# Windowed attention with sinks, then a gated MLP block: half of the spatial weights turned by DMA, and another PSUM bank for one unit

## The chip, the cores and the metric

The kernel runs on one core of one Trainium2 chip. The time is the device time of one launch in microseconds (us), and lower is better. Several executions are timed; one more is recorded by the hardware profiler, and every view of the profile below is of that one execution.

The engines have short names: PE is TensorE (matmuls and transposes), PEld its weight loads, DVE is VectorE, ACT is ScalarE, POOL is GpSimd, and SP is SyncE, which in this kernel only issues DMAs. SPq is SP's queue.

## The reference

```python
# attention: B=4, H=8, S=768, D=64, 4 sink columns, window 128
scores = q @ k.T / sqrt(D)
keep   = (pos[None, :] < 4) | ((rel >= 0) & (rel < 128))     # rel = row - column
a      = softmax(where(keep, scores, -1e9))
x      = (a @ v).transpose(0, 2, 1, 3).reshape(B, S, 512)
# gated MLP
h      = gelu_tanh(x @ w_in)                  # 512 -> 1024
u, v   = h[..., :512], h[..., 512:]
v_n    = (v - mean(v)) / sqrt(var(v) + 1e-6) * g_ln
v_s    = einsum('ts,bsd->btd', w_sg, v_n) + b_sg[None, :, None]   # w_sg is 768 x 768
out    = x + (u * v_s) @ w_out
```

The spatial product sums over positions s. TensorE needs the summed index on the partitions, so w_sg, which is read with t on the partitions, has to be turned once: wsgT holds it with s on the partitions, as six blocks of 128 rows by 768 columns.

## The kernel before

All tiles have 128 partitions. S is six tiles (NT = 6, HT = 3). Attention is done for pairs of heads: 4 batches of 4 pairs are 16 pairs, n = 0 to 15 (HP = 4). The MLP is done for a batch ("block" b) when its four pairs are through.

The order of the work is written out by hand in the loop over n (line 571); each engine executes its own instructions in that order. In an iteration the scores of pair n are made in three groups g (`score`, line 249), exponentiated by ACT and masked by DVE (`keep_band`, line 266); meanwhile the value products of pair n - 1 are done (`values`), and the keys and queries of pair n + 1 are turned by PE (`keys`, `queries`). At the end of an iteration SP gets the loads of pair n + 3 (`load_qk`, line 75).

When n is a multiple of 4, `hidden` (line 424) runs the first half of the MLP of the batch just finished, n // 4 - 1: six units `hidden_v` (line 327), each four matmuls and a GELU on ACT, and statistics on DVE; then eight units `hidden_u` (line 339). What follows, the spatial products (`spatial`, eight units of six matmuls, line 376) and the projections (`project`, six units, line 391), is put into a list, `fillers`, and `spread` takes them out one or two at a time between the attention work of the next iterations. For block 0 the list begins with the six units `spatial_weights` (line 177) that turn w_sg. So this happens once, at n = 5. Of the eight spatial units the first four (n = 0 in the code of `spatial`) read the first 384 columns of wsgT and the last four the second 384.

w_sg is loaded at n = 4 by two DMAs of POOL's queue (line 168), the first for t tiles 0 to 2, the second for 3 to 5. For pairs 4 to 14 that are not the last of their batch, x is turned by a DMA transpose from SP's queue (line 321); otherwise by PE (`columns`, line 283).

PSUM has eight banks: `ps_s` for scores (two buffers of two banks), `ps_a` for values (one), `ps_t`, tag "tp", for the transposes of keys and queries (one), and `ps_m`, tag "mm", two buffers shared by everything else: `hidden_v`, `hidden_u`, `spatial`, `project`, `columns` and `spatial_weights`. A unit that takes a buffer waits until the unit before last in the same pool has been read out.

Of the kernel before, what the change touches and what calls it, by code (L numbers as in the profile page):

```python
# [8 lines left out]
F32 = mybir.dt.float32  # L9
# [8 lines left out]
def kernel(  # L18
# [14 lines left out]
    nc = tc.nc  # L33

    B, H, S, Dh = q.shape
# [5 lines left out]
    NT = S // 128  # L41
    HP = H // 2
# [13 lines left out]
    ps_t = ctx.enter_context(tc.tile_pool(name="ps_t", bufs=1, space=PSUM))  # L56
    ps_m = ctx.enter_context(tc.tile_pool(name="ps_m", bufs=2, space=PSUM))
# [3 lines left out]
    HT = NT // 2  # L61
# [13 lines left out]
    def load_qk(n):  # L75
        b, hp = divmod(n, HP)
        pair = []
        for src, name in ((k, "k_sb"), (q, "q_sb")):
            dst = loads.tile([128, 2, NT, 64], F32, name=name)
            nc.sync.dma_start(out=dst, in_=src[b, 2 * hp:2 * hp + 2].rearrange(  # L80
                "h (p t) d -> p h t d", t=NT))
            pair.append(dst)
        qk[n] = pair
# [71 lines left out]
    wsg_sb = consts.tile([128, NT, S], BF16, name="wsg_sb")  # L155
    w_out_sb = consts.tile([128, KU, DM], BF16, name="w_out_sb")
    wsgT = consts.tile([128, NT, S], BF16, name="wsgT")
# [16 lines left out]
            nc.gpsimd.dma_start(out=w_out_sb,  # L174
                                in_=moe_w_out.rearrange("(c p) f -> p c f", p=128))

    def spatial_weights(si):
        wps = ps_m.tile([128, NT, 128], BF16, name="wps", tag="mm")
        for ti in range(NT):
            nc.tensor.transpose(wps[:, ti, :],  # L180
                                wsg_sb[:, ti, 128 * si:128 * (si + 1)], iden)
        nc.vector.tensor_copy(wsgT[:, si, :], wps.rearrange("p t q -> p (t q)"))  # L182

    packed, qTs, exps, avs = {}, {}, {}, {}
    x_sb, xT = {}, {}
# [1 line left out]
    def repack(n, eng):  # L187
        packed[n] = []
        for src, name in zip(qk.pop(n), ("k_bf", "q_bf")):
            flat = work.tile([128, NT, 128], BF16, name=name)  # L190
            eng.tensor_copy(flat.rearrange("p t (h d) -> p h t d", h=2), src)  # L191
            packed[n].append(flat)
# [134 lines left out]
    def hidden_v(b, j):  # L327
        if j == 0:
            v_alls[b] = work.tile([128, NT, DF], F32, name="v_all", tag="v_all", bufs=1)
            mvs[b] = small.tile([128, NT, 2], F32, name="mv", bufs=2)  # L330
        h_ps = ps_m.tile([128, 512], F32, name="hv", tag="mm")
        for c in range(KD):
            nc.tensor.matmul(h_ps, xT[b][:, c, 128 * j:128 * (j + 1)],  # L333
                             w_in_sb[:, c, DF:], start=(c == 0), stop=(c == KD - 1))
        nc.scalar.activation(out=v_alls[b][:, j, :], in_=h_ps, func=AF.Gelu_apprx_tanh)  # L335
        st = small.tile([128, 6], F32, name="st")
        nc.vector.bn_stats(out=st, in_=v_alls[b][:, j, :])  # L337
        nc.vector.bn_aggr(out=mvs[b][:, j, :], in_=st)

    def hidden_u(b, f, n):  # L340
        if f == 0 and n == 0:
            uTs[b] = work.tile([128, KU, S], BF16, name="uT")
        h_ps = ps_m.tile([128, 512], F32, name="hu", tag="mm")
        for c in range(KD):
            nc.tensor.matmul(h_ps[:, 0:NH], w_in_sb[:, c, 128 * f:128 * (f + 1)],  # L345
                             xT[b][:, c, NH * n:NH * (n + 1)],
                             start=(c == 0), stop=(c == KD - 1))
        nc.scalar.activation(out=uTs[b][:, f, NH * n:NH * (n + 1)],  # L348
                             in_=h_ps[:, 0:NH], func=AF.Gelu_apprx_tanh)
# [3 lines left out]
    def inverse_root(b):  # L353
        rstd = rstds[b] = small.tile([128, NT], F32, name="rstd", bufs=2)
        var = small.tile([128, NT], F32, name="var", bufs=2)
        tmp = small.tile([128, NT], F32, name="tmp", bufs=2)
        nc.vector.tensor_scalar_add(var, mvs[b][:, :, 1], 1e-6)
        nc.vector.tensor_single_scalar(tmp.bitcast(I32), var.bitcast(I32), 1,
                                       op=ALU.logical_shift_right)
        nc.vector.tensor_scalar(out=rstd.bitcast(I32), in0=tmp.bitcast(I32),  # L360
                                scalar1=-1.0, scalar2=float(0x5F3759DF),
                                op0=ALU.mult, op1=ALU.add)
        for _ in range(3):
            nc.vector.scalar_tensor_tensor(out=tmp, in0=rstd, scalar=-0.5, in1=rstd,
                                           op0=ALU.mult, op1=ALU.mult)
            nc.vector.tensor_mul(tmp, tmp, var)
            nc.vector.scalar_tensor_tensor(out=rstd, in0=tmp, scalar=1.5, in1=rstd,
                                           op0=ALU.add, op1=ALU.mult)

    def normalise(b, j):  # L370
        if j == 0:
            vns[b] = work.tile([128, NT, DF], BF16, name="vn")
        nc.vector.tensor_scalar(out=vns[b][:, j, :], in0=v_alls[b][:, j, :],
                                scalar1=mvs[b][:, j, 0:1], scalar2=rstds[b][:, j:j + 1],
                                op0=ALU.subtract, op1=ALU.mult)
# [35 lines left out]
    def project_halves(b, t, queue):  # L411
        project(b, t, queue, nc.scalar, slice(DM // 2, DM))
        project(b, t, queue, nc.vector, slice(0, DM // 2))

    fillers = []
# [6 lines left out]
    def hidden(b, between, queue=nc.sync):  # L422
        def step():
            if between:
                between.pop(0)()

        for j in range(NT):
            hidden_v(b, j)
            for _ in range(min(j + 1, 2)):
                step()  # L430
        for i in range(2 * KU):
            hidden_u(b, i % KU, i // KU)
            if i == 0:
                inverse_root(b)
            elif i <= NT:
                normalise(b, i - 1)
        if b == 0 and queue is nc.sync:
            fillers.extend(lambda si=si: spatial_weights(si) for si in range(NT))
        for n in range(2):
            for f in range(KU):  # L440
                fillers.append(lambda f=f, n=n: spatial(b, f, n))
        for t in range(NT):
            if b == B - 1 and t == NT - 1:
                fillers.append(lambda t=t: project_halves(b, t, queue))
            else:
                by = nc.scalar if b == B - 2 else nc.vector
                fillers.append(lambda t=t, by=by: project(b, t, queue, by))
# [123 lines left out]
    for n in range(NP):  # L571
        if n + 2 < NP:
            repack(n + 2, G)
            load_v(n + 2)
        load_weights(n)
        late = half_valued == n - 1

        def value(i):
            if n > 0 and (i >= HT or not late):
                values(n - 1, i)  # L580

        points = (HT + 1) * ((HP - n) % HP)

        def spread(left):
            if n > HP * (B - 1):
                fill(1 if left > 2 or (left == 1 and n < NP - 1) else 0)
            else:
                fill(-(-len(fillers) // (points + left)))

        for g in range(HT):  # L590
            if g == HT - 1 and n % HP == 0 and n > 0:
                sinks(n)
            if n + g > 0:
                score(n, g)
            if g < 2 and not late:
                for i in range(HT * g, HT * (g + 1)):
                    value(i)
            if g == 0 and n > 0 and n + 1 < NP:
                keys(n + 1)
                if n < HP:  # L600
                    queries(n + 1, A, ps_m, "mm")
            if g == 0 and late:
                for i in range(HT, NT):
                    value(i)
                spread(HT + 1)
            if g == HT - 1 and n % HP == 0 and n > 0:
                columns(n - 1)
            keep_band(n, g)
            if g == 1 and late:
                spread(HT)  # L610
            if g == 1 and n + 1 < NP and n >= HP:
                queries(n + 1, A, ps_t, "tp")
            if g == 2 or not late:
                spread(HT + 1 - g)
        if n + 3 < NP:
            load_qk(n + 3)
        if n % HP > 0 or n == 0:
            sinks(n)
        if n == 0:
            keys(1)  # L620
            queries(1, A, ps_m, "mm")
        if 0 < n < HP:
            columns(n - 1)
        spread(1)
        if n % HP == 0 and n > 0:
            fill(len(fillers))
            hidden(n // HP - 1, [lambda i=i: values(n, i) for i in range(HT)])
            half_valued = n
# [58 lines left out]
```

## Time and profile before

| | |
|---|---|
| timed runs | 178.34, 180.28, 180.62 us; median 180.28 |
| profiled execution | 178.66 us; its span, from the first to the last instruction, 176.9 us |
| mean granted TensorE clock | 0.992 |
| busy PE, DVE, ACT, POOL | 157.6, 144.9, 118.7, 58.5 us |
| PE transposes of w_sg (line 180) | 36, from 44.6 to 49.9 us |
| DVE copies out of them (line 182) | 6 of 548 ns |
| hidden_v matmuls (line 333) | 96, 379 ns each from start to end |
| DMA transposes of x (line 321) | 9, from 45.7 to 138.7 us |

In the lines of the profile, `wsgT<-wps` means that wsgT is written from wps, x12 is a number of instructions, and times are us from the start of the span. In a timeline a row is start, length, engine, line, operation, and in brackets the idle time of the engine just before and what ended it. In the chain of waits a row is start, length, what. Matmuls are pipelined: one that lasts 219 ns from start to end may be followed by the next after a fraction of that. Several instructions in one row may overlap in the same way.

### The profile page before, as it was taken

The numbers are of one execution on the slowest core, as the hardware profiler recorded it, in microseconds if no ns is written. First come the engines' busy times: TensorE is split into PE (matmuls) and PEld (weight loads), VectorE is DVE, ScalarE is ACT, GpSimd is POOL, SyncE is SP. The second block draws the span as 40 slices with busy tenths as digits, with TensorE's granted clock in tenths as the row PEclk, the third lists the DMA queues.
The fourth block names the chain that finished last, engine by engine and source line by source line (L and its number), as shares of the span: only waits on it lengthen the run. The fifth ranks groups of instructions, "written<-read, shape, count | busy, mean of one in ns | idle before, by whom it ended". The sixth has DMA issues, their size and how long they took to land.

```text
span 176.9 us, 3760 instructions
## 1 busy us (share of the span) xinstructions
PE 157.6 (89%) x1418; PEld 88.6 (50%) x1418; DVE 144.9 (82%) x359; ACT 118.7 (67%) x168; POOL 58.5 (33%) x98
## 2 busy tenths in 40 slices
PE   0769779899689999999999999999999999999970
PEld 0446556445546555455555545455465454546430
DVE  6664989699889999798989999699999949858950
ACT  2488999877928677667978678777996756640000
POOL 8549999960043070624025070461010000000000
PEclk9999999999999999999999999999999999999996
DMA  5999999999957739799086969986202241011072
GB/s 157 267 272 284 238 269 267 214 205 229 158 173 48 203 69 228 281 254 81 4 222 40 214 179 199 375 114 44 44 4 46 48 180 59 0 69 55 0 290 73
DMA packets 47974, 27.24 MB, mean 154 GB/s; under 512 B 33680, under 2 KB 44944, under 8 KB 47952
## 3 DMA queue, kind: packets, MB, share of 16 engines
q0 software_dynamic: 27904, 6.31, 37.8%
q1 hardware_dynamic: 19504, 20.26, 37.5%
q10 hardware_dynamic: 544, 0.39, 0.7%
q8 instruction: 12, 0.20, 0.5%
q14 instruction: 10, 0.08, 0.2%
HBM read 24.81 MB, written 6.29 MB: 176 GB/s over the span
## 4 chain that ended last, share of the span: by engine, by line
PE 58%; DVE 20%; ACT 10%; issue 5%; POOL 3%; DMA 2%; POOLq 0%; DVEq 0%; ACTq 0%
PE vs L383 12%; PE o_ps L397 10%; PE hu L345 10%; PE hv L333 9%; ACT ex L264 5%; PE sc L260 5%; DVE ex L271 4%; PE cps L197 4%; PE av L305 3%; DVE gv L386 3%; DVE x L316 2%; DVE st L337 2%; DMA k_sb<-in_k_dram 2%; ACT kT L204 2%; DVE gT L389 2%
## 5 line engine op out<-in xcount | busy, mean ns | idle before, releaser
L264 ACT ACTIVATE ex<-sc 128x1024 bf16<-128x1024 f32 (+1 forms) x48 | 45.6, 958 | 15.2 <-PE sc L260 15.1
L383 PE MATMUL vs<-wsgT,vn 128*128 128x384 bf16 x192 | 35.5, 326 | 0.5 <-DVE wsgT L182 0.2
L191 POOL CAST k_bf<-k_sb 128x768 bf16<-128x768 f32 x15 | 13.7, 910 | 40.9 <-DMA k_sb<-in_k_dram 37.5
L397 PE MATMUL o_ps<-w_out_sb,gT 128*128 128x512 bf16 (+1 forms) x100 | 24.2, 370 | 0.3 <-DVE o_sb L401 0.2
L271 DVE TENSOR_TENSOR ex<-ex,mask 128x1024 bf16<-128x1024 bf16 x32 | 22.8, 717 | 1.8 <-ACT ex L264 1.7
L383 PEld LDWEIGHTS <-vn 128*128 128x128 bf16 x192 | 17.8, 98 | 12.4 <-issue 1.8
L333 PE MATMUL hv<-w_in_sb,xT 128*128 128x512 bf16 x96 | 22.3, 379 | 1.4 <-ACT v_all L335 0.9
L345 PE MATMUL hu<-xT,w_in_sb 128*128 128x384 bf16 x128 | 23.2, 324 | 0.1
L260 PE MATMUL sc<-qT,kT 64*128 64x256 bf16 x192 | 19.0, 280 | 2.5 <-DVE qT L240 1.3
L386 DVE SCALAR_TENSOR_TENSOR gv<-vs,g_sb,b_bc 128x384 bf16<-128x384 f32 x32 | 19.5, 611 | 1.8 <-PE vs L383 1.7
L337 DVE BATCH_NORM_STATS2 st<-v_all 128x6 f32<-128x512 f32 x24 | 16.3, 678 | 4.9 <-ACT v_all L335 4.9
L348 ACT ACTIVATE uT<-hu 128x384 bf16<-128x384 f32 x32 | 15.7, 490 | 6.5 <-PE hu L345 6.3
L335 ACT ACTIVATE v_all<-hv 128x512 f32<-128x512 f32 x24 | 14.1, 597 | 7.5 <-PE hv L333 7.5
L316 DVE TENSOR_TENSOR x<-av,inverses 128x384 bf16<-128x384 f32 x32 | 17.8, 558 | 1.1
L305 PE MATMUL av<-v_sb,ex 128*128 128x65 bf16 x192 | 18.2, 198 | 0.6 <-DVE x L316 0.5
L305 PEld LDWEIGHTS <-ex 128*128 128x128 bf16 x192 | 14.5, 100 | 7.8 <-issue 3.1
L345 PEld LDWEIGHTS <-w_in_sb 128*128 128x128 bf16 x128 | 12.4, 97 | 10.7 <-issue 2.9
L87 POOL DMA_DIRECT2D v_sb<-in_v_dram x16 | 16.6, 1036 | 0.0
L308 PE MATMUL av<-v_sb,ex 128*128 128x65 bf16 x160 | 16.5, 197 | 0.0
L214 POOL COPY sk<-kT 64x4 bf16<-64x4 bf16 x30 | 7.1, 237 | 27.6 <-ACT kT L204 26.7
L333 PEld LDWEIGHTS <-xT 128*128 128x128 bf16 x96 | 9.1, 97 | 12.0 <-issue 1.2
L408 ACT COPY o_act<-o_ps 128x512 f32<-128x512 f32 (+1 forms) x7 | 3.7, 549 | 15.7 <-PE o_ps L405 15.7
(83 smaller groups left out, 249.7 us busy)
## 6 DMA issues: line engine op xcount, KB each, us to landing
k_sb<-in_k_dram SPq DMA_DIRECT2D x15, 384.0 KB, 5.1
q_sb<-in_q_dram SPq DMA_DIRECT2D x15, 384.0 KB, 5.9
out_dram<-o_sb SPq DMA_DIRECT2D x17, 256.0 KB, 3.3
v_sb<-in_v_dram POOLq DMA_DIRECT2D x16, 192.0 KB, 6.8
out_dram<-o_act SPq DMA_DIRECT2D x6, 256.0 KB, 2.0
wsg_sb<-in_moe_w_sg_dram POOLq DMA_DIRECT2D x2, 576.0 KB, 9.7
w_in_sb<-in_moe_w_in_dram POOLq DMA_DIRECT2D x4, 256.0 KB, 8.5
w_out_sb<-in_moe_w_out_dram POOLq DMA_DIRECT2D x1, 512.0 KB, 10.4
```

What stands on the lines that cost most here:

```text
L87: nc.gpsimd.dma_start(out=v_bufs[n % NV][:, :, :, 0:64], in_=v[b, 2 * hp:2 * hp + 2].rearrange("h (t p) d -> p h t d", p=128))
L260: nc.tensor.matmul(sc[:, hl, w:w + n_q], kT[rows, 128 * j:128 * (j + 1)], qT[rows, 128 * j:128 * j + n_q], start=True, stop=True)
L264: nc.scalar.activation(out=part, in_=sc[:, :, 0:w], func=AF.Exp, scale=scale)
L271: nc.vector.tensor_mul(part, part, m)
L305: nc.tensor.matmul(av[:, m, hl, :], probs(i, hl, 0), v_sb[:, hl, i, :], start=(m == 0 and hl == 0), stop=False)
L316: nc.vector.tensor_mul(x_sb[b][:, hp, HT * c:HT * (c + 1), :].rearrange("p i (h d) -> p i h d", h=2), av[:, :, :, 0:64], rcp.to_broadcast( ...
L333: nc.tensor.matmul(h_ps, xT[b][:, c, 128 * j:128 * (j + 1)], w_in_sb[:, c, DF:], start=(c == 0), stop=(c == KD - 1))
L337: nc.vector.bn_stats(out=st, in_=v_alls[b][:, j, :])
L345: nc.tensor.matmul(h_ps[:, 0:NH], w_in_sb[:, c, 128 * f:128 * (f + 1)], xT[b][:, c, NH * n:NH * (n + 1)], start=(c == 0), stop=(c == KD - 1))
L383: nc.tensor.matmul(vs[:, 0:NH], vns[b][:, si, 128 * f:128 * (f + 1)], wsgT[:, si, cols], start=(si == 0), stop=(si == NT - 1))
L386: nc.vector.scalar_tensor_tensor(out=gv, in0=vs[:, 0:NH], scalar=g_sb[:, f:f + 1], in1=b_bc[:, cols], op0=ALU.mult, op1=ALU.add)
L397: nc.tensor.matmul(o_ps, gTs[b][:, c, rows], w_out_sb[:, c, cols], start=(c == 0), stop=(c == KU - 1 and whole))
```

## The change

Three edits go together. `spatial_weights` now turns one t tile of w_sg per unit, for all six s tiles, and DVE writes it as 128 columns in each of the six blocks of wsgT; formerly a unit turned one s tile for all t. Only t tiles 0 to 2 are turned so, in three units. Tiles 3 to 5 are turned by three DMA transposes from SP's queue, issued at the end of iteration n = 4, behind the loads of pair 7. And the first `hidden_v` unit of blocks 0, 1 and 2 takes its PSUM buffer from `ps_t` in place of `ps_m`. The fillers of block 0 become 17 in place of 20; at n = 5 the first two spatial units now stand right behind the three turning units, the first of them ahead of the sinks' matmul (line 275). From n = 6 on PE's instructions have the order that they had.

```diff
-    def spatial_weights(si):
+    def spatial_weights(ti):
         wps = ps_m.tile([128, NT, 128], BF16, name="wps", tag="mm")
-        for ti in range(NT):
-            nc.tensor.transpose(wps[:, ti, :],
+        for si in range(NT):
+            nc.tensor.transpose(wps[:, si, :],
                                 wsg_sb[:, ti, 128 * si:128 * (si + 1)], iden)
-        nc.vector.tensor_copy(wsgT[:, si, :], wps.rearrange("p t q -> p (t q)"))
+        nc.vector.tensor_copy(wsgT[:, :, 128 * ti:128 * (ti + 1)], wps)
+
+    def turn_spatial_weights():
+        for ti in range(HT, NT):
+            nc.sync.dma_start_transpose(out=wsgT[:, :, 128 * ti:128 * (ti + 1)],
+                                        in_=wsg_sb[:, ti, :])
...
-        h_ps = ps_m.tile([128, 512], F32, name="hv", tag="mm")
+        pool, tag = (ps_t, "tp") if j == 0 and b < B - 1 else (ps_m, "mm")
+        h_ps = pool.tile([128, 512], F32, name="hv", tag=tag)
...
-        if b == 0 and queue is nc.sync:
-            fillers.extend(lambda si=si: spatial_weights(si) for si in range(NT))
         for n in range(2):
+            if b == 0 and n == 0 and queue is nc.sync:
+                fillers.extend(lambda t=t: spatial_weights(t) for t in range(HT))
             for f in range(KU):
                 fillers.append(lambda f=f, n=n: spatial(b, f, n))
...
         if n + 3 < NP:
             load_qk(n + 3)
+        if n == HP:
+            turn_spatial_weights()
```

## The prediction

> **What bounds the kernel now.** I read the page first, for the whole span, then the chain of waits in order of time, then each engine's timeline at the four places that the edits touch.
>
> ```profile
> PE 157.6 (89%) x1418; PEld 88.6 (50%) x1418; DVE 144.9 (82%) x359; ACT 118.7 (67%) x168; POOL 58.5 (33%) x98
> PE 58%; DVE 20%; ACT 10%; issue 5%; POOL 3%; DMA 2%; POOLq 0%; DVEq 0%; ACTq 0%
> ```
>
> PE carries 58% of the chain, but 42% is elsewhere, so an edit is worth what its own stage says. The spatial weights are turned in one stage, 44 to 52 us (pair n = 5). The chain there, in order of time (start, length, what):
>
> ```profile
> 45.28 1.02 ACT ex L264
> 46.30 0.69 ACT kT L204
> 46.99 0.94 ACT ex L264
> 47.95 0.69 DVE ex L271
> 48.64 0.93 DVE wsgT L182 x2
> 49.58 0.47 DVE ex L271
> 50.04 0.48 DVE wsgT L182
> 50.56 2.11 PE vs L383 x12
> ```
>
> Until 47.93 the end is set by ACT's exponentials, then by DVE: one mask, two copies of turned weights, a mask, two more copies (the last two overlap), and only then can PE begin the spatial units. PE waits twice inside its transposes; the bracket is its idle time and the releaser:
>
> ```profile
> 46.22 0.96 PE L180 MATMUL wps<-iden,wsg_sb 128*128 128x128 bf16 x12 [0.48 <-DVE wsgT L182]
> 49.16 0.96 PE L180 MATMUL wps<-iden,wsg_sb 128*128 128x128 bf16 x12 [1.35 <-DVE wsgT L182]
> ```
>
> The second edit touches the starts of blocks 0, 1 and 2. PE's timeline shows one wait at each, by three different causes:
>
> ```profile
> 34.16 3.61 PE L333 MATMUL hv<-w_in_sb,xT 128*128 128x512 bf16 x16 [0.58 <-ACT v_all L335]
> 73.65 1.02 PE L333 MATMUL hv<-w_in_sb,xT 128*128 128x512 bf16 x4 [0.43 <-DVE o_sb L401]
> 113.07 3.18 PE L333 MATMUL hv<-w_in_sb,xT 128*128 128x512 bf16 x14 [0.36 <-ACT v_all L335]
> ```
>
> After the third the chain leaves PE for DVE and stays there until about 141:
>
> ```profile
> 112.42 0.60 ACT v_all L335
> 113.05 0.71 DVE st L337
> ...
> 121.88 2.83 DVE vn L373 x6
> ```
>
> The queue that gets the new transposes is SP's. It is empty from 27 to 45.7; the two lines after are what would now stand behind them:
>
> ```profile
> 26.61 0.37 SPq L80 DMA_DIRECT2D q_sb<-in_q_dram  x1
> 45.73 1.48 SPq L321 DMA_TRANSPOSE xT<-x  x1
> 47.31 0.53 SPq L80 DMA_DIRECT2D k_sb<-in_k_dram  x1
> ```
>
> **The spatial weights.** Removed: 18 of 36 PE transposes and three of six DVE copies. A transpose lasts 219 ns but twelve are issued between 44.58 and 45.34, 63 ns each, so 18 x 63 ns = 1.1 us of PE; the three copies are 3 x 0.47 us (548 ns each, overlapping). What this is worth on the path: the first two copies still end before the first mask, unchanged. The third still stands behind the second mask, which waits for the exponential that ends at 47.93. Mask 47.95 to 48.64, copy from 48.56 to 49.11, and PE starts the first spatial unit at 49.16 instead of 50.56. Twelve matmuls take 2.04 us up to the next score matmul (50.56 to 52.60); the sinks' matmul, formerly ahead of them, now stands between the two units and adds 0.22 (58.24 to 58.46). The next pair's first score is at 49.16 + 2.04 + 0.22 = 51.42 instead of 52.60: **1.18 us**. From there PE's list is the same as before and the timeline shows it without a wait until 73, so the shift is kept. DVE, busy 9.0 to 9.4 of each 10 us there, is not left behind: its first gated product moves from 51.74 to about 50.3. The new copies write six runs of 128 columns; no row shows that form. The nearest, 548 ns (contiguous) and 558 ns (the x product, strided), agree; I take 548. Up to 690 ns (the o_sb addition), 0.14 more for the one copy on the path, is the upper bound.
>
> TensorE: Matmul & The Clock Gate of the Trainium skill (Part 4: PE-mode transpose) gives about 275 ns per transpose in a kernel. By that figure, end to end, 18 would be 4.95 us of PE; the trace's issue distance of 63 ns contradicts it, and the path above does not use either.
>
> **The three DMA transposes.** They have the shape of the nine on line 321: 1.2 to 1.5 us of SP each, and these landing times (minimum, median, maximum, us), followed by those of the spatial weights' own two loads:
>
> ```profile
> DMA to landing us min/median/max: 2.8/2.8/4.7
> DMA to landing us min/median/max: 8.7/9.7/10.7
> ```
>
> The second load is issued at about 32.5, so it lands by 43.2, and the first transpose waits for that. With 1.48 us each the issues end at 47.6, the last begun at 46.2 and landed by 46.2 + 4.7 = 50.9 (49.0 by the median). Their first reader is the fifth spatial unit, at 57.26 before, 55.7 after all shifts: 4.8 us of cover. Queued behind them on SP are the x transpose of pair 4 (45.73, now 47.6; wanted by block 1 at 73) and the loads of pair 8, about 1.9 us later. POOL's cast of those keys goes from 51.09 to 53; PE wants it at 60.2. I cost all that at nothing; without cover each microsecond late is one on PE.
>
> **The first unit in the transpose bank.** It leaves the two-buffer pool, so each later unit of that block looks back one unit less. Block 0: unit 2 need not wait for the first GELU and follows the values at 33.42; unit 3 waits for the second GELU's end, 34.61, and starts at 34.66, formerly 34.16 + 0.86 = 35.02. Gain **0.36**. DVE's list to 45 does not move, but ACT's does, since the table load follows the last GELU, and ACT sets the 45 to 48 us stage. Block 1: the first unit need not wait for the o_sb addition: **0.43**, and PE runs on to the next stage. Block 2: PE gains about 0.3, but the DVE chain starts with the first GELU, whose table load is where it was: **0**. The wait that is added, for the bank's last reader, is met: the query copy ends at 31.05 and the unit starts at 31.07; the two others are a microsecond or more early. If the ends are wrong this edit is worth between 0 and 0.58 + 0.43 + 0.36 = 1.37.
>
> **Sum.** 1.18 + 0.36 + 0.43 = 1.97 us. The profiled execution took 178.66, span 176.9 and 1.76 around it; it becomes 176.7, span 174.9. The runs shown are 178.34, 180.28 and 180.62; with 178.66 the middle of the four is 179.47, so the median expected for the changed kernel is 179.47 - 1.97 = **177.5**.
>
> **Rivals.** (a) *The bank only moves the wait*: the waits at 34.16 and 73.65 come back one unit later on ACT. For: both later waits in the list are on GELU. Against: GELU takes 0.60 of each 0.86 us unit. Gain 1.18, time 178.3.
> (b) *The whole stage drains*: all PE waits of 44 to 52 go (0.48 + 1.35 + 0.22) with the 1.1 of transposes, 3.15 and 0.79 from the banks, time 175.5. For: DVE has less to do. Against: the third copy is queued behind a mask that waits for ACT.
> (c) *The turned half is late*, the slower side. Place: the fifth spatial unit, PE at 55.7. It costs more than the whole gain once the last transpose lands after 57.7. If the three are served one after another at 4.7 they land at 43.2 + 14.1 = 57.3, a wait of 1.6 and 179.1, no loss; if sharing the engines doubles that, 43.2 + 28.2 = 71.4, a wait of 15.7 and 193.2. For: the DMA engines are over 90% busy until about 47. Against: the x transpose at 45.73 landed in 3.2 in that traffic. VectorE: DVE Perf Modes of the Trainium skill (The three transpose paths) speaks for it: 1309 ns for one 128x128 block by DMA against 390 by TensorE. By that figure 18 blocks in a row would end at 66.8, and the time would be 188.6. The trace disagrees: six blocks landed in 2.8 to 4.7.
> (d) *It does not do what it says*: the first copies would have to wait for the DMA half, since both write one tile. The instruction lists put no such wait there; no chance of its own.
>
> **How the numbers follow.** Forecast 0.68, (a) 0.16, (b) 0.10, (c) 0.06. A measurement of this kernel tells about 2%, 3.6 us, from no change: its runs spread by 1.3%. The forecast is a gain of 1.1%, of which scatter carries 0.10 beyond 2% and 0.01 beyond the other side; with (b) faster is 0.20, with (c) slower 0.07, and 0.73 stays within. The range goes from the lowest run less the stage's 3.15, 175.2, to the median shown with no gain, 180.3; (c) is left out.
>
> **What would show it.** PE's first spatial unit at about 48.8 (49.16 less 0.36) and the sixth pair's first score near 51.1; three SP transposes from about 43, landed by 51; no PE wait at the fifth unit; no o_sb wait at block 1's start, about 71.7; block 2's DVE chain as long as before, starting 2 us earlier. A PE wait on DMA near 55.7, or an unchanged 50.6, makes the forecast wrong.

## The result, and the profile after

The changed kernel takes 177.60 us (median of 20 runs, 176.25 to 179.82), the kernel before 179.35 (20 runs, 178.14 to 181.94) on the same chip. The ratio is 0.9888, with a 95% interval of 0.9859 to 0.9917: a gain of 1.1%, or 2.0 us (1.5 to 2.5). Repeated later as e3 it was 0.9892 (0.9839 to 0.9945). The forecast was 177.5.

The ratios leave out the executions that are over 1.5% longer than the fastest of their kernel, so that a ratio is not always the quotient of the two medians. In the profiled execution of the changed kernel (179.16 us, span 177.3, mean clock 0.983) the granted clock is halved for 3.4 us. Where that matters below, e10's profile stands in for it: the same program with one more output buffer, span 174.2, clock 0.998.

First the changed kernel's page: the row of busy times, the shares of the chain by engine, and the granted clock in 40 slices of 4.4 us each.

```profile
PE 158.0 (89%) x1400; PEld 88.0 (50%) x1400; DVE 144.2 (81%) x356; ACT 118.6 (67%) x168; POOL 59.7 (34%) x98
PE 51%; DVE 21%; DMA 13%; ACT 7%; issue 4%; POOL 1%; ACTq 0%; POOLq 0%
PEclk9999999999969999999999999999999999999997
```

The 18 transposes and three DVE copies are gone. DMA has 13% of the chain where it had 2%; the page puts it down to a load of v_sb (6%) and to outputs (4% and 2%), and names no transpose of w_sg. One slice, the twelfth, ran at a lower clock. Now the chain of waits through the stage of the spatial weights:

```profile
46.62 0.94 ACT ex L269
...
47.58 0.69 DVE ex L276
48.28 0.48 DVE wsgT L182
...
48.80 2.08 PE vs L389 x6
```

This is the chain that was forecast: exponential, second mask, one copy instead of two pairs with a mask between them, and the first spatial unit at 48.80 (forecast 48.8). PE's timeline at the places of the two edits (the bracket is the idle time just before and what ended it):

```profile
32.52 0.22 PE L310 MATMUL av<-v_sb,ex 128*128 128x65 bf16 x2 [0.28 <-DMA v_sb<-in_v_dram]
...
33.75 3.66 PE L339 MATMUL hv<-w_in_sb,xT 128*128 128x512 bf16 x16
...
46.23 0.49 PE L180 MATMUL wps<-iden,wsg_sb 128*128 128x128 bf16 x6 [0.86 <-DVE wsgT L182]
...
48.80 2.08 PE L389 MATMUL vs<-wsgT,vn 128*128 128x384 bf16 x6 [1.36 <-DVE wsgT L182]
...
73.79 1.03 PE L339 MATMUL hv<-w_in_sb,xT 128*128 128x512 bf16 x4
```

The three waits that the prediction named at the starts of blocks 0, 1 and 2 are gone (block 2 has no bracket at 112.86). In block 0 another stands now, the first row: 0.28 us for a load of v_sb. Such a wait varies by execution, from none (before, e2, e5) to 0.95 us (e12). PE's wait ahead of the spatial unit is as long as before, only earlier. But this unit takes 2.08 us for six matmuls, and block 1 begins no earlier than before (73.79 against 73.65). The windows of 48 to 50 and 50 to 52 us say why: granted clock 0.64 and 0.51. In e10 at full clock the same two rows are

```profile
48.66 1.14 PE L389 MATMUL vs<-wsgT,vn 128*128 128x384 bf16 x6 [1.36 <-DVE wsgT L182]
...
71.38 1.03 PE L339 MATMUL hv<-w_in_sb,xT 128*128 128x512 bf16 x4
```

the score of pair 6 is at 50.92 (52.60 before; forecast 51.1), and block 1 begins 2.27 us earlier than before. SP's timeline, and the landing times of the three transposes (minimum, median, maximum), again of the changed kernel:

```profile
43.17 5.01 SPq L186 DMA_TRANSPOSE wsgT<-wsg_sb  x3
48.23 1.29 SPq L326 DMA_TRANSPOSE xT<-x  x1
...
DMA to landing us min/median/max: 4.4/5.1/5.7
```

The x transpose went from 45.73 to 48.23, the keys from 47.31 to 49.61. The last of the three is issued from 45.85 on and landed by 51.6 at the latest; the fifth spatial unit starts at 57.25 without a wait. In e10 the last is issued from 47.2 on and landed by 52.9, and the fifth unit starts at 55.57, again without a wait: a cover of 2.7 us where 4.8 were forecast.

One wait is new. It stands at block 3's start, 90 us behind the edits. ACT copies out the last projection of block 2; the two lines are of before, ACT and then PE:

```profile
144.67 0.58 ACT L408 COPY o_act<-o_ps 128x512 f32<-128x512 f32 x1 [0.87 <-PE o_ps L405]
144.42 5.36 PE L333 MATMUL hv<-w_in_sb,xT 128*128 128x512 bf16 x24
```

and these of the changed kernel:

```profile
145.23 0.58 ACT L414 COPY o_act<-o_ps 128x512 f32<-128x512 f32 x1 [1.42 <-DMA out_dram<-o_act]
145.87 4.48 PE L339 MATMUL hv<-w_in_sb,xT 128*128 128x512 bf16 x20 [0.40 <-ACT o_act L414]
```

The copy is the fourth into three buffers, so it waits for an output DMA. That DMA lands 3.35 us after its issue where it took 2.03 before, the copy is late, and PE waits for the PSUM buffer which it frees. From the first values' matmul of block 3 to the first of `hidden_u`: 150.18 - 144.44 = 5.74 us, before 149.62 - 144.42 = 5.20.

### The profile page after: what moved, and what is told of

It is laid out like the page before. It is cut to its first block, busy times and chain, and to the rows that moved or that the text cites. A ratio compares the mean times of both kernels' runs of the same rounds, so it can differ in the third digit from the quotient of the medians.

```text
span 177.3 us, 3728 instructions
## 1 busy us (share of the span) xinstructions
PE 158.0 (89%) x1400; PEld 88.0 (50%) x1400; DVE 144.2 (81%) x356; ACT 118.6 (67%) x168; POOL 59.7 (34%) x98
## 4 chain that ended last, share of the span: by engine, by line
PE 51%; DVE 21%; DMA 13%; ACT 7%; issue 4%; POOL 1%; ACTq 0%; POOLq 0%
PE vs L389 13%; PE o_ps L403 9%; PE hu L351 6%; DMA v_sb<-in_v_dram 6%; PE hv L339 5%; PE sc L265 5%; DMA out_dram<-o_sb 4%; DVE st L343 3%; PE cps L202 3%; ACT ex L269 3%; PE av L310 3%; DVE ex L276 3%; DVE gv L392 2%; DVE vn L379 2%; DMA out_dram<-o_act 2%
## 5 line engine op out<-in xcount | busy, mean ns | idle before, releaser
L389 PE MATMUL vs<-wsgT,vn 128*128 128x384 bf16 x192 | 37.1, 335 | 1.7 <-DVE wsgT L182 1.4
L196 POOL CAST k_bf<-k_sb 128x768 bf16<-128x768 f32 x15 | 13.1, 874 | 41.1 <-DMA k_sb<-in_k_dram 22.2
L339 PE MATMUL hv<-w_in_sb,xT 128*128 128x512 bf16 x96 | 22.8, 379 | 0.4 <-ACT o_act L414 0.4
L219 POOL COPY sk<-kT 64x4 bf16<-64x4 bf16 x30 | 7.6, 255 | 25.1 <-ACT kT L209 24.3
L196 POOL CAST q_bf<-q_sb 128x768 bf16<-128x768 f32 x15 | 14.1, 938 | 3.8 <-PE hu L351 1.9
```

Of the source, the lines that this page charges most:

```text
L339: nc.tensor.matmul(h_ps, xT[b][:, c, 128 * j:128 * (j + 1)], w_in_sb[:, c, DF:], start=(c == 0), stop=(c == KD - 1))
L389: nc.tensor.matmul(vs[:, 0:NH], vns[b][:, si, 128 * f:128 * (f + 1)], wsgT[:, si, cols], start=(si == 0), stop=(si == NT - 1))
```

## The experiments

Every kernel is compared with the kernel before on the same chip. Ratios are followed by their 95% interval.

### e1 and e2: each edit alone

e1 is the changed kernel with the bank put back, e2 the kernel before with the bank only:

```diff
 e1, against the changed kernel
-        pool, tag = (ps_t, "tp") if j == 0 and b < B - 1 else (ps_m, "mm")
-        h_ps = pool.tile([128, 512], F32, name="hv", tag=tag)
+        h_ps = ps_m.tile([128, 512], F32, name="hv", tag="mm")
 e2, against the kernel before
-        h_ps = ps_m.tile([128, 512], F32, name="hv", tag="mm")
+        pool, tag = (ps_t, "tp") if j == 0 and b < B - 1 else (ps_m, "mm")
+        h_ps = pool.tile([128, 512], F32, name="hv", tag=tag)
```

> The change with the first hidden_v unit left in the two-buffer pool. Theory P (path): the weights' edit alone is worth 1.18 us, so about 0.993 of the kernel before; PE's first spatial unit at 49.16, the PE waits at the starts of blocks 0 and 1 (0.58 on GELU, 0.43 on the o_sb addition) are back. Theory B (the bank does it all, the turned weights are hidden anyway): 1.000. Theory A (additive with more than the path, all PE waits of the stage go): 3.15 us less, 0.982.

> The kernel before with only the first hidden_v unit of blocks 0, 1 and 2 in the transpose bank. Theory P: 0.36 in block 0 and 0.43 in block 1, nothing in block 2, since DVE sets the end there: 0.8 us less, 0.9956. Rival B: the waits only move to a later unit, 1.000 (and then the weights' edit carries all of the 1.12%). Rival C: block 2 counts too, 1.1 us, 0.994. In the trace: PE waits less before the third unit of block 0, none on the o_sb addition in block 1, and block 2's first vn at the same distance from its first GELU as before.

Measured: e1 178.09 us (12 runs), 0.9937 (0.9902 to 0.9973); e2 178.13 (12), 0.9952 (0.9919 to 0.9985). On 178.85 that is 1.13 us and 0.86 us. They add up to 1.11%, and the change gave 1.12%. No gain at all (1.000) lies outside both intervals, and 0.982 outside e1's; 0.994 in e2, with block 2 counted, is not told from 0.9956. In e1 the waits for GELU are back at blocks 0 and 2 (0.18 and 0.36 us), but at block 1 none is. In e2 block 1 starts without a wait. At block 0 the wait moves one unit on, to the place and size that were forecast; the row is PE's:

```profile
34.27 2.10 PE L334 MATMUL hv<-w_in_sb,xT 128*128 128x512 bf16 x9 [0.28 <-ACT v_all L336]
```

This fourth unit starts 3.55 us after the block's first (30.72); forecast 34.66 - 31.07 = 3.59, before 3.95.

### e3: the change again

> The changed kernel itself, for a profile at full clock and beside the two halves on the same chip. Theory P: 0.989, and the two halves multiply to it (0.993 x 0.9956 = 0.989). PE's first spatial unit at about 48.8 in this profile too; if PE keeps its clock from 48 to 53 us, the score of pair 6 starts at about 51.1, where the profile with a lowered clock had 52.6.

Measured: 177.39 (6 runs), 0.9892.

### e4: the other half by PE too

The second three tiles are turned by PE as well, behind the first four spatial units, and there is no DMA transpose. `spread` is set, in lines left out here, so that at n = 5 it takes out as many units at each place as in the change.

```diff
-            if b == 0 and n == 0 and queue is nc.sync:
-                fillers.extend(lambda t=t: spatial_weights(t) for t in range(HT))
+            if b == 0 and queue is nc.sync:
+                fillers.extend(lambda t=t: spatial_weights(t)
+                               for t in range(HT * n, HT * (n + 1)))
...
-        if n == HP:
-            turn_spatial_weights()
```

> The change without DMA transposes: all six tiles of w_sg are turned by PE, per output tile, three units ahead of the spatial units as in the change and the other three only behind the fourth spatial unit, where their columns are needed; the bank edit is kept. Theory P (what pays is that only three turning units stand in front of the spatial units): the 1.18 us are still gained at n = 5, and 18 transposes of 63 ns are given back later on PE, 1.1 us: about 0.995, first spatial unit at 48.8 as in the change. Theory D (the DMA's taking over of PE and DVE work is the gain): the same time and reason, but then the three copies cost DVE 1.4 us more too, 0.996 to 0.998. Rival E (the late units are hidden, PE had room): 0.989, as the change; then DMA transposes were not needed.

Measured: 180.58 (12 runs), 1.0087 (1.0050 to 1.0124), slower than before; all three forecasts missed. The stage at 48 us is the change's (48.56 and 50.82). The late units stop PE in the next iteration:

```profile
57.35 0.50 PE L180 MATMUL wps<-iden,wsg_sb 128*128 128x128 bf16 x6 [1.14 <-DVE wsgT L182]
58.75 1.14 PE L389 MATMUL vs<-wsgT,vn 128*128 128x384 bf16 x6 [0.90 <-DVE wsgT L182]
```

The third unit finds both PSUM buffers unread, and the spatial unit waits for a copy that stands behind DVE's last mask. So a unit of six transposes costs what its copy's place in DVE's queue costs, not its 0.4 us of PE. Against this placing, DMA for the second half is worth 2.0% (1.0087 over 0.9890); against e2, which turns all six by PE ahead of the spatial units, it is 0.6%. Other placings were not tried.

### e5 and e6: PE's wait ahead of the first spatial unit

e5 takes that wait away. The third turning unit gets the idle bank of the values, all three units go first in the iteration, and their copies stand ahead of the masks:

```diff
     def spatial_weights(ti):
-        wps = ps_m.tile([128, NT, 128], BF16, name="wps", tag="mm")
+        pool, tag = (ps_a, "av") if ti == 2 else (ps_m, "mm")
+        wps = pool.tile([128, NT, 128], BF16, name="wps", tag=tag)
...
-                spread(HT + 1)
+                fill(HT) if n == HP + 1 else spread(HT + 1)
...
-            if g == 1 and late:
+            if g == 1 and late and n != HP + 1:
...
-                spread(HT + 1 - g)
+                fill(1) if n == HP + 1 else spread(HT + 1 - g)
```

e6 leaves the wait but fills it with seven small matmuls whose result the next matmul overwrites:

```diff
+        for si in range(7 if b == 0 and f == 0 and n == 0 else 0):
+            nc.tensor.matmul(vs[:, 0:NH], vns[b][:, si % NT, 0:128],
+                             w_in_sb[:, 0, 0:NH], start=True, stop=True)
```

> The change with another order at n = 5: the third turning unit follows the first two at once, in the values' PSUM bank, so that all three copies stand ahead of DVE's masks; the spatial units keep their places behind the last scores and behind the sinks. Theory P (what ends last in front of the spatial units is the third copy, held back by a mask that waits for ACT): the copy ends at 47.1 instead of 48.75, PE's first spatial unit starts near 47.2 instead of 48.8 and pair 6's first score near 49.6 instead of 51.1. DVE's first gated product comes behind the last mask, at about 49.5 instead of 50.2, so that 0.7 to 1.5 us are kept: 0.981 to 0.985 of the kernel before. Rival F (ACT sets this stage, and a later first mask holds it back): 0.989 or more, as the change. Rival G (the gain is taken back by DVE further on): first spatial unit early as in P, time 0.987 to 0.989.

> The change with seven idle matmuls (data that are there, overwritten at once by the unit's own first matmul) ahead of PE's first spatial unit, 7 x 0.17 = 1.2 us in a wait of 1.36. Theory K (PE's low share of busy time from 45 to 49 us lets the granted clock fall to one half for some 3 us in part of the executions, which then take 2 us longer): no or few executions with a mean clock under 0.989 where the change has 8 of 26, and no slice under full clock in the profile; those at full clock unchanged at 0.989. Rival L (the clock falls for another cause): the same share of executions with a low clock, about a third, at the same place, and the same ratio. Rival M (the seven matmuls delay the unit): up to 0.2 us more, 0.990.

Measured: e5 176.35 (6 runs), 0.9845 (0.9793 to 0.9896), faster than the kernel before; its interval overlaps the change's. Theory P's places hold: the wait of 1.36 us is gone (one of 0.72 us, for DVE's x product, stays ahead of the third turning unit), and the spatial unit starts 1.6 us earlier than in the change:

```profile
45.42 1.48 DVE L183 COPY wsgT<-wps 128x768 bf16<-128x768 bf16 x3
47.17 1.15 PE L390 MATMUL vs<-wsgT,vn 128*128 128x384 bf16 x6
```

The first line is DVE's, all three copies in one go ahead of the masks. The next score is at 49.44, 1.5 us before e10's. e6: 177.93 (12 runs), 0.9944 (0.9913 to 0.9975). Its profile has the real unit at 48.59 and the score at 50.85, clock 1.00 from 44 to 58 us, which is the forecast's stage. Theory K has the clock right, since none of the 12 runs is under 0.989, but not the time: the ratio is worse than the change's by 0.6%, with intervals that just touch, and why stays open.

### e7 and e8: all by DMA, and the transposes late

```diff
 e7
-        for ti in range(HT, NT):
+        for ti in range(NT):
             nc.sync.dma_start_transpose(out=wsgT[:, :, 128 * ti:128 * (ti + 1)],
...
 e8
-        if n == HP:
+        if n == HP + 1:
             turn_spatial_weights()
```

e7 also takes the three turning units out of the fillers, and two calls of `spread` at n = 5, so that the spatial units stay where the change has them.

> All six tiles of w_sg by DMA transposes, no PE transposes and no DVE copies of them; spatial units where the change has them. Theory P: the first three are issued from about 40.5 (first weight load landed) at 1.3 to 2.3 us each and land up to 5.7 us after their issue, by 49 to 50, so that PE's first spatial unit waits on DMA until then, 48.8 in the change: 0 to 1.2 us more than the change, 0.989 to 0.996 of the kernel before. Rival D (less PE and DVE work is what counts): the unit starts at about 47.4 behind the last scores and the time is 1.4 us less than the change's, 0.981.

> The three DMA transposes one iteration later, behind the loads of pair 8 in SP's queue. Theory P (they are hidden by some 4 us of cover, and no more): issued from about 48.4, done issuing at 52 to 53.5, landed by 54 to 58; the fifth spatial unit, due at 55.7, waits 0 to 2 us on DMA: 0.989 to 1.000. Rival H (SP's place does not matter, since what is moved is small): no wait and 0.989.

Measured: e7 183.14 (3 runs), 1.0201 (1.0132 to 1.0270); both theories missed. SP's timeline, then PE's:

```profile
42.20 13.14 SPq L186 DMA_TRANSPOSE wsgT<-wsg_sb  x6
54.27 2.08 PE L389 MATMUL vs<-wsgT,vn 128*128 128x384 bf16 x6 [6.43 <-DMA wsgT<-wsg_sb]
```

Six transposes hold SP for 13.1 us; single issues took 1.3 to 5.1 us, landings 2.8 to 10.5. The first three are issued at 42.20, 43.62 and 48.72, and PE waits 6.4 us for them. This is rival (c)'s mechanism, a turned part that comes late, with no cover; on top the clock is at half rate from 49.6 to 59.8 us. The change is spared it by the 2.7 us of cover, not by fast transposes.

e8: 178.97 (9 runs), 1.0006 (0.9969 to 1.0044): the whole gain is gone. Not by the wait that was feared: the transposes are issued from 49.18 on and land in 3.2 to 4.6 us, and PE has no wait between 52 and 76 us. Six of the nine runs have a mean clock under 0.99, but the other three, 178.5 on average, are hardly better. The profile is 0.7 us behind e10's at the first spatial unit (49.37 against 48.66); this stems from the load of v_sb in block 0 (a wait of 0.92 us against 0.46, and the row behind it at 33.13 against 32.43), ahead of the first thing that the edit moves. It is 1.0 behind at block 1's start and 2.0 at block 2's. In between PE waits 0.43 and 0.30 us for DVE, where e10 has no wait: one DVE product takes 0.95 us in place of 0.36 (at 91.84 us) and one mask 1.33 in place of 0.68 (at 102.04), each beside a cast on POOL (from 91.75 and 102.01). The new wait of block 3 is there too (ACT waits 1.81 us). So the loss is measured, but that it comes from the place in SP's queue is not shown.

### e9 to e11: the late output

The theory: the new wait of block 3 gives back part of the gain. A fourth buffer for ACT's outputs removes it; e9 is e5 with it, e10 the change, e11 the kernel before.

```diff
-            o_sb = small.tile([128, DM], F32, name="o_act", bufs=3)
+            o_sb = small.tile([128, DM], F32, name="o_act", bufs=4)
```

> The reordered kernel of e5 (0.9845) with a fourth buffer for the outputs that ScalarE copies. Theory F (a new wait behind the change): at block 3's start the fourth ScalarE copy waits for the first output DMA, which lands 4.1 us after its issue instead of 2.2, and the values' matmuls of block 3 wait for ScalarE, 1.07 us in e5. With a fourth buffer the copy no longer waits: no such releaser in the profile, hv to hu of block 3 back from 6.4 to about 5.2 us, 0.6 to 1.1 us less than e5, ratio 0.979 to 0.981. Rival R: the wait is covered, or the next thing (the block's last outputs, its DVE chain) sets the end anyway: 0.9845 as e5.

> The change with a fourth buffer for the outputs that ScalarE copies, nothing else. Theory F: the 0.5 to 0.7 us between the first values' and the first other half's matmuls of block 3 that the change loses (5.8 us in its profiles against 5.2 before) come back, ratio 0.985 to 0.987 (the change itself 0.9888 and 0.9892). Rival R: the late output lands under something else that sets the end, 0.989.

> The kernel before with the fourth buffer, nothing else: the control of e9 and e10. Theory F: its first output lands 2.2 us after its issue, the fourth copy waits for PE and not for a DMA, so 1.000. Rival: the buffer is worth its gain whatever is turned by DMA, 0.996 or less.

Measured: e9 175.54 (6 runs), 0.9807 (0.9758 to 0.9856), the fastest of all; e10 0.9872 (0.9819 to 0.9925; 12 runs, median 178.60, lowest 176.00); e11 178.97 (9), 0.9994 (0.9957 to 1.0031). ACT and PE in e10:

```profile
142.04 0.58 ACT L414 COPY o_act<-o_ps 128x512 f32<-128x512 f32 x1 [0.83 <-PE o_ps L411]
141.84 5.34 PE L339 MATMUL hv<-w_in_sb,xT 128*128 128x512 bf16 x24
```

The copy waits for PE again, as in before. From these rows and their like, with the longest landing of ACT's outputs around block 3's start:

| kernels | w_sg transposes by DMA | longest landing, us | values to other half in block 3, us |
|---|---|---|---|
| before, e2, e4, e11, e12 | 0 | 2.2 | 5.2 |
| the change | 3 | 3.5 | 5.7 |
| e1, e3, e6, e8 | 3 | 3.4 to 3.9 | 5.6 to 6.1 |
| e5 | 3 | 4.1 | 6.4 |
| e7 | 6 | 3.1 | 5.2 |
| e9, e10 (four buffers) | 3 | 3.5, 3.4 | 5.2 |

So the wait is shown, and so is its cure: 0.5 us in the change, 1.2 in e5. The profiles of e6 (three buffers) and e10 (four) say the same of the path: at the starts of blocks 1, 2 and 3, counted from block 0's, they are within 0.15 us of each other, and at block 3's `hidden_u` e10 is 0.5 us ahead. e9's profile is not ahead of e5's there (147.05 against 146.95), since its block 3 begins 1.3 us later for a reason that was not found. In the times the cure is only likely: e9 is 0.7 us below e5 and e10 0.3 below the change, and each pair of intervals overlaps.

The landings stay late in e9 and e10, and the DMA records of the traces show what the late outputs meet. The page of the profile counts 12 packets of a queue q8 of the kind "instruction", 16 KB each, and in all 14 profiles one of them lies near the first of these outputs. In the five kernels without w_sg transposes it starts 0.3 to 0.9 us before the output is issued and has ended at most 0.5 us after that, ahead of the output's first data (0.86 us after the issue). In the eight with three it starts 0.55 to 1.54 us after the issue and takes 0.9 to 1.5 us. An output ends with 16 packets of 4 bytes. In those eight 15 of them come 1.5 to 1.7 us after the issue, as all 16 do in the five; the last comes after 2.7 to 3.4 us, 0.7 to 1.0 us behind the end of the q8 packet. In e7 the q8 packet starts 2.27 us after the issue: the first two outputs land in 2.0 and 2.2 us, and the third in 3.1.

So one of the output's 16 parts is late, each time shortly behind this packet, and nothing here ties it to the order in SP's queue. Why the packet comes later was not tested. PE has 18 transposes fewer in these kernels and 36 fewer in e7, and the packet is the later the fewer there are, which would fit a load of PE's instructions; no run separates this from the DMA transposes.

### e12: the bank of block 2 alone

```diff
+        pool, tag = (ps_t, "tp") if j == 0 and b == 2 else (ps_m, "mm")
+        h_ps = pool.tile([128, 512], F32, name="hv", tag=tag)
```

> The kernel before with the first unit of block 2 alone in the transpose bank; blocks 0 and 1 and the spatial weights as before. The forecast's step: PE's wait of 0.36 us at 113 goes, but block 2's VectorE chain starts with the first GELU, whose table load is where it was, so the start of block 3 does not move: 1.000. Rival: the 0.36 us of PE reach the end, 0.998. The two are told apart by block 2's and block 3's first values in the profile, since 0.002 is within the scatter of the times.

Measured: 178.47 (9 runs), 0.9981 (0.9938 to 1.0025), which decides nothing. In the profile PE's wait is gone, and DVE's statistics still begin when the first GELU is out. From block 2's first matmul to block 3's it is 33.84 us, against 34.03 before and 34.01 in e11, where the wait stands; with all banks moved, e2, it is 34.1. Nothing here exceeds what profiles of the same code differ by.

## Why the prediction was right, and where it was not

The steps are best read at full clock and from block 0's first values' matmul on (31.07 before, 30.84 in e10, 30.72 in e2, 30.94 in e11), since what lies ahead of it scatters by 0.3 us. Gains against before, so counted:

| up to | forecast | e10 | e6 | e11, the order of before |
|---|---|---|---|---|
| pair 6's first score | 1.54 | 1.45 | 1.58 | 0.04 less |
| block 1's first values | 1.97 | 2.04 | 2.17 | 0.30 |
| block 3's first values | 1.97 | 2.35 | 2.47 | 0.12 |
| block 3's first `hidden_u` | 1.97 | 2.37 | 1.86 | 0.14 |

The first row is 21.53 us before (52.60 - 31.07) and 20.08 in e10; the others go in the same way. e6 is the change at full clock with its three output buffers, but for the seven matmuls in PE's wait.

**The weights, 1.18 us.** Right in place and size: e1 gave 1.13 us (0.5 to 1.75), and the chain shows the step that was argued, the one copy behind the second mask.

**The bank, 0.36 + 0.43 + 0.** Right in sum: e2 gave 0.86 (0.27 to 1.45). Block 0's part is 0.41 us at the first spatial unit (49.80 - 30.72 against 50.56 - 31.07), with the remaining wait where it was put. Block 1's 0.43 is too much: that wait stands in the one profile of before only. e11, e12 and e1, where this unit still takes its buffer from `ps_m`, show no wait there. From the start of the last eight projection matmuls to the first values' matmul it is 2.31 us before, 1.96 to 1.97 in those three, and 1.72 to 1.73 in e2, the change and e10: the bank is worth 0.24 us there, and the rest is in e11's 0.30 too. Block 2's zero has nothing against it, since e12's interval holds it. Rival (a), that the waits only move, is wrong: in e2 one of the three moved, at half its length, and a bank worth nothing lies outside e2's interval.

**The DMA transposes.** "Landed by 50.9" and "4.7" were too low: up to 5.7 us. The row that the bound came from is of x transposes issued one at a time, but that this is the reason is not shown, since e8's three in a row landed in 3.2 to 4.6. The cover took the difference. By an estimate from the Trainium skill's figure in VectorE: DVE Perf Modes (The three transpose paths), 1309 ns a block, 18 blocks would have landed 23.6 us after the first issue, at 66.7; the trace has all of them by 51.6. Rival (c) is thereby out for the change, but e7 shows that its mechanism is real.

**What the sum lacked.** "So the shift is kept" was read from PE's list up to 73 us, and no step looked at block 3's start. There the change loses 0.5 us to the late output, a term that was missing. "I cost all that at nothing", on what is queued behind the transposes on SP, did hold: the x transpose and the keys came later, and PE did not wait for them.

**Where luck helped.** The sum was 0.2 us too high for block 1 and lacked the 0.5 us at block 3. Against that, the profiles gain 0.3 us between blocks 1 and 3 (2.35 - 2.04 in e10), which no step foresaw and which was not traced to an edit. In e6 the whole comes to 1.86 us (1.72 against e11), the medians say 1.75 and the ratio 2.0: the stages of the weights and of block 0 were forecast rightly, and that the total agrees to 0.1 us is partly luck.

**Rival (b), the whole stage drains**, is not what happened, since the 1.36 us wait stayed in the change. That most of it can be drained is shown by e5, in which the third copy is moved ahead of the masks: what (b) lacked was DVE's order, not less work on DVE.

**Prices given in the experiments** failed where a unit of transposes (e4) was priced by PE's time, and a transpose (e7) by an issue of 1.3 to 2.3 us. In both the price is set by a queue: DVE's for the copies, SP's for the issues.

## What to carry to other kernels

Work that moves to a DMA queue is priced by the queue: six transposes held SP for 13.1 us in e7, where one alone took 1.2 to 1.5 before. Follow a shift to the end of the span, and look at each buffer whose reuse waits for a DMA: the change lost 0.5 us at one, 90 us behind its edits. A short unit whose result another engine must copy out is worth what the copy's place in that engine's queue is worth: moving the third copy ahead of the masks (e5) brought another 1.5 us in the stage. A wait that one profile shows is not yet a price: block 1's 0.43 us was worth 0.24. Spread a transposition over two engines as far as there is cover for the slower one, and no further: together with the bank, half by DMA gained 1.1%, and all of it lost 2.0%.

## What the runs showed of the hardware

**The clock.** In the changed kernel's profile the granted clock falls in the middle of the span. Windows of the stage (start and end, length, busy us and count of PE, PEld, DVE, ACT and POOL, granted clock, DMA engines' share, GB/s):

```profile
48.00:50.00 2.00, 1.20 (x4) 0.55 (x4) 1.30 (x3) 0.96 (x2) 0.00 (x0) 0.64 1.26 258
50.00:52.00 2.00, 2.00 (x7) 0.88 (x6) 0.98 (x2) 0.59 (x1) 0.00 (x0) 0.51 0.79 167
```

At half rate these clocks mean 1.44 us of the first window and 1.96 of the second, together 3.4 us, in which a matmul of 326 ns took up to 524. PE had idled 0.86 us and 1.36 us shortly before, with matmuls between. TensorE: Matmul & The Clock Gate of the Trainium skill (Part 1: The HAM clock gate) has the rate halved after an idle window of about 3.4 us and restored after as long a busy one. The length agrees; the cause only in part, since no idle stretch here reached 1.4 us, and e10's profile, with waits of 0.73 and 1.36 us, kept its full clock.

The traces show where such waits fall. Four profiles have the drop. In the change, e1 and e3 it begins 30.72 us after the clock's first rise (17.83 to 48.55 us in the change), nine times 3.41 us, and lasts 3.41 us; in e7 it begins after ten times 3.41 and lasts three times that. Counted in steps of 3.41 us from that rise, every step with under 1.5 us of PE work is followed by the drop (1.44 us in the change, 1.35 in e1, 0.77 in e7), and none with 1.9 or more (1.96 before, 2.05 in e10, 2.01 in e11). In between it went both ways: 1.78 us in e3 with the drop, 1.75 in e8 without. This fits waits that cost clock when they fall into one step and not when two steps share them.

In e5 and e9 (no wait of 1.36 us there) and e6 (wait filled) none of the 24 timed runs had a mean clock under 0.99; in the change 6 of 20 had, in e10 6 of 12, in e8 6 of 9. But e11, with the waits of before, had none in 9 either. That idling in this stage calls the drop forth is suggested, not shown.

**Issue and landing of DMA transposes.** One x transpose alone held SP for 1.2 to 1.5 us before, and for up to 2.1 in the change. Three of w_sg in a row took 5.0 us in the change (up to 2.33 each), 4.0 in e8 and 6.5 in e9; six took 13.1 us (up to 5.06 each). Landings were 2.8 us in the median and 4.7 at most for the x transposes before, up to 5.7 for three of w_sg in the change (7.1 in e9), and up to 10.5 for six.
